# S4 convolution beside hedgehog linear attention on one core: state parameters and their power tables built in two halves of the channels

## The chip, the cores and the metric

The kernel runs on one core of a Trainium2 chip. The metric is the device time of one execution in microseconds (us). The median of three runs of the kernel before is 230.67 us. Five engines work side by side, each through its own list of instructions: TensorE (PE, matmuls and transposes), VectorE (DVE), ScalarE (ACT), GpSimd (POOL) and SyncE (SP), which here only issues DMAs. An instruction waits for the data and the buffers that it needs, and whatever stands behind it in the same engine's list waits with it.

## The reference

Two independent parts write side by side into an output of 2048 x 896 in bf16.

```python
# A: linear attention, 16 heads of 28, x is 2048 x 448
q, k, v = split(x @ wqkv)
phi(t) = concat(softmax(t @ w_phi), softmax(-(t @ w_phi)))
kv, z  = sum_s phi(k) v, sum_s phi(k)
a      = (phi(q) kv / (phi(q) z + 1e-6)) @ wo
# B: state space convolution, 448 channels d, 256 states n, u is 2048 x 448
dt     = exp(log_dt)
P      = exp(dt (A_re + i A_im) l),  l = 0..2047
K[d,l] = Re sum_n C[d,n] P[d,n,l] dt B[d,n]
y      = irfft(rfft(pad(u)) * rfft(pad(K)))[:2048] + u * Dskip
out    = concat(a, y)
```

## The kernel before, in words

Everything is tiled by hand. Code appends operations to a program (`prog.add`, engine letters E for PE, V for DVE, A for ACT, G for POOL, S for DMAs) and four lists at the end of the file decide the rest: ORDER is the order in which all 1040 operations are issued, so each engine's own order too; PLACES gives every SBUF buffer its address; SLOTS gives every PSUM use its bank (of eight); PICKS says for each copy, scaling or squaring whether ACT or DVE does it, and for each DMA whether it is issued on SP's queue or ACT's. No scheduler stands behind them. Buffers and banks are reused, so an operation that writes one waits for the readers of what lay there.

Part B has these stages. The 448 channels are taken in four quarters `qt` of 112 (224 columns, QC, for two groups of 128 states each; NCOL = 896 columns for all).

- Raw parameters: `load_raw` (L262) brings the six arrays A, B, C (real and imaginary) as 112 x 4 x 256, one DMA of 224 KB each; A_re goes on ACT's queue (L289). `Wqk` (L298) comes as one DMA and the constants of the signal spectrum, `G1` (L309), as another.
- States: `to_states` (L332) multiplies with the diagonal of dt on PE and lays states on partitions, into two PSUM banks. From A come AT and TH (decay and angle), from four products of C and B comes CR.
- Powers: for k in (128, 16, 8, 32, 64), `amp[k]` is an exponential on ACT, `cs[k]` two sines on ACT, and `PW[k]` their product on DVE, 1792 wide in f32. `PW[256]` is squared out of `q128`, and CB is CR times `PW[8]`. `K0` is a sum over CR for l = 0. All of it is done once, for all four quarters.
- Signal spectrum (`signal_spectrum(b)`, L420-440): PE reverses rows of u, ACT or DVE evacuates, DVE adds and subtracts (`ab`), PE multiplies with G1, ACT casts into `sg`, and a DMA stores it to DRAM (`SUd`, L249).
- Tables of a quarter (`tables(qt)`): `rotations` (sines) and `dampings` (exponentials) on ACT, `hi_tables`, `damp` and `far` on DVE, `build_k` on PE with casts by ACT or DVE, `scatter_k` by DMA through DRAM (`KTd`).
- `kernel_spectrum(qt)` on PE with casts, then `conv(qt)`: products on DVE, `finish` on DVE or `finish_pe` on PE, `inverse` on PE, an evacuation and a store to the output. The inverse of one `(qt, b)` makes two evacuations of 448 columns and two stores of 112 KB.

Part A (`fold_weights`, `key_side`, `query_side(sc)`) runs in between; its exponentials and evacuations are ACT's largest work, and x comes transposed by 16 DMAs on SP's queue (`dma_t`, L245). Sines and exponentials need different tables on ACT: where the list goes from the one to the other, a table load stands (L203 and L206). Helpers record all operations, so the profile shows their lines: L186 DVE tensor_tensor, L206 ACT activations, L214 copies and casts, L229 matmuls, L249 DMAs.

Of the kernel before, what the change touches and what calls it, by code (L numbers as in the profile page):

```python
# [10 lines left out]
F32 = mybir.dt.float32  # L11
ACT = mybir.ActivationFunctionType
ALU = mybir.AluOpType
# [116 lines left out]
def kernel(  # L130
# [116 lines left out]
    def dma(eng, o, i):  # L247
        e = {"S": nc.sync, "Q": nc.scalar}[prog.queue()]
        prog.add("S", lambda: e.dma_start(out=o, in_=i))  # L249
# [29 lines left out]
    def load_u(b):  # L279
# [9 lines left out]
    prog.add("S", lambda: nc.scalar.dma_start(  # L289
        out=raw["Are"].rearrange("p (u j) n -> p u (j n)", u=2),  # L290
        in_=srcs["Are"].rearrange("(u p j) n -> p u (j n)", u=2, j=2)))
    dma("S", PID, P_d)
    for nm in ("Aim", "Cre", "Bre", "Cim", "Bim"):
        load_raw(nm)
# [3 lines left out]
    Wqk = sb([112, 4, 2 * D_MODEL])  # L298
    WV = sb([128, 4, D_MODEL])
    dma("S", Wqk, wq3[:, :, 0:2 * D_MODEL])  # L300
# [8 lines left out]
    G1 = sb([128, 2, 4, 512])  # L309
    dma("S", G1, G_d)  # L310
# [12 lines left out]
    def from_states(bs):  # L323
        return view(psum[:, bs[0], 0:1], [512 * (bs[1] - bs[0]), 2], [56, 8], [1, 56])

    def by_states(v):
        return view(v, [56, 2], [112, 8], [1, 56])

    def to_states(bs, terms):
        items = []  # L330
        for j in range(4):
            for nch in range(2):  # L332
                at = 224 * (j // 2) + 56 * (j % 2)
                o = view(psum[:, bs[nch], at:at + 1], [112, 2], [1, 56])
                items += acc(o, [(t[:, j, 128 * nch:128 * nch + 128], d[:, j, :]) for t, d in terms])
        mms(items)

    AT = sb([128, 2, NCOL])
    TH = sb([128, 2, NCOL])
    bA, bT = prog.banks(2), prog.banks(2)  # L340
    for nm, b, dst in (("Are", bA, AT), ("Aim", bT, TH)):
        to_states(b, [(raw[nm], DG)])
        for nch in range(2):
            o0, o1 = (view(dst[:, part, 56 * nch:56 * nch + 1], [112, 8], [1, 2], [2, 28]) for part in range(2))
            i = view(psum[:, b[nch], 0:1], [56, 8], [28, 2], [1, 28])
            copy(o0, i)
            sub(o1, i, o0)
    prods = {}
    for a, b in (("Cre", "Bre"), ("Cim", "Bim"), ("Cre", "Bim"), ("Cim", "Bre")):
        prods[a + b] = sb([112, 4, SSM_N])  # L350
        mul(prods[a + b], raw[a], raw[b])

    LOWP = (128, 16, 8, 32, 64)
    PW = {k: sb([128, 2, NCOL]) for k in (8, 16, 32, 64, 128, 256)}
    amp = {k: sb([128, NCOL], F32) for k in LOWP}
    cs = {k: sb([128, 2, NCOL], F32) for k in LOWP}
    q128, q256 = (sb([128, 2, NCOL], F32) for _ in range(2))
    CR = sb([128, 2, NCOL])
    K0 = sb([128, D_MODEL])
    ones = sb([128, 128])  # L360
    for k in LOWP:
        af(by_states(amp[k]), from_states(bA), ACT.Exp, scale=float(k))
    for part, terms in enumerate(([("CreBre", DG), ("CimBim", DGN)], [("CreBim", DG), ("CimBre", DG)])):
        bs = prog.banks(2)
        to_states(bs, [(prods[n], d) for n, d in terms])
        copy(by_states(CR[:, part, :]), from_states(bs))
    mset(ones, 2.0 ** -17)
    (b_,) = prog.banks(1)
    mms([it for qt in range(4) for it in acc(
        view(psum[:, b_, 112 * qt:112 * qt + 1], [14, 8], [7, 2], [1, 7]),  # L370
        [(ones, view(CR[:, 0, QC * qt + 56 * nch:QC * qt + 56 * nch + 1], [7, 8], [112, 2], [1, 7]))
         for nch in range(2)])])
    copy(K0, psum[:, b_, 0:D_MODEL])
    for k in LOWP:
        af(by_states(cs[k][:, 0, :]), from_states(bT), ACT.Sin, scale=float(k), bias=bias_hp)
        af(by_states(cs[k][:, 1, :]), from_states(bT), ACT.Sin, scale=float(-k if k == 8 else k))
        mul(PW[k] if k != 128 else q128, cs[k], amp[k].unsqueeze(1).to_broadcast([128, 2, NCOL]))
        if k == 128:
            copy(PW[128], q128)
    s2 = sb([128, 2, NCOL], F32)  # L380
    square(s2, q128)
    sub(q256[:, 0, :], s2[:, 0, :], s2[:, 1, :])
    stt(q256[:, 1, :], q128[:, 0, :], -2.0, q128[:, 1, :], ALU.mult, ALU.mult)
    copy(view(PW[256][:, 0, 0:1], [56, 32], [1, 2], [2, 28]), view(q256[:, 0, 0:1], [56, 32], [28, 2], [1, 28]))
    CB = sb([128, 2, NCOL])
    TM = sb([128, 2, 2, NCOL])
    mul(TM, CR.unsqueeze(1).to_broadcast([128, 2, 2, NCOL]), PW[8].unsqueeze(2).to_broadcast([128, 2, 2, NCOL]))
    add(CB[:, 0, :], TM[:, 0, 0, :], TM[:, 1, 1, :])
    sub(CB[:, 1, :], TM[:, 0, 1, :], TM[:, 1, 0, :])
# [6 lines left out]
    def fold_weights(which):  # L396
        for cp in range(2):
            p = bank16(*prog.banks(1), [112, 2, D_MODEL])
            c0 = which * D_MODEL + 224 * cp
            transposes([(p[:, k, 112 * j:112 * j + 112], Wqk[:, j, c0 + 112 * k:c0 + 112 * k + 112], id112)  # L400
                        for k in range(2) for j in range(4)])
            copy(wT[:, which, 2 * cp:2 * cp + 2, :], p)
# [14 lines left out]
    def signal_spectrum(b):  # L417
# [9 lines left out]
        for cp in range(2):  # L427
            for st in range(2):
                k = 2 * cp + st
                sg = sb([128, 4, 4, 112])  # L430
                for mp in range(2):
                    items = []
                    bs = prog.banks(2)
                    for k2 in range(2):
                        mt = 2 * mp + k2
                        items += acc(psum[:, bs[k2], 0:D_MODEL],
                                     [(G1[:, cp, jt, 128 * mt:128 * mt + 128], ab[:, cp ^ st, jt, :])
                                      for jt in range(4)])
# [30 lines left out]
    def args(src, qt):  # L469
        cols = slice(qt * QC, (qt + 1) * QC)  # L470
# [8 lines left out]
    def rotations(qt):  # L479
        T = sb([128, 2, 7, QC])  # L480
        p0, far_ = args(TH, qt)
# [12 lines left out]
    def dampings(qt):  # L494
        A = sb([128, 21, QC])
        p0, far_ = args(AT, qt)
# [13 lines left out]
    def damp(W, A, T, qt, x0, w):  # L510
        scaled(A[:, 2:21:3, x0:x0 + w], A[:, 1:20:3, x0:x0 + w], -1.0)
        for part in (1, 0):
            copy(view(W[:, part, 1, x0:x0 + 1], [56, w // 56], [2, 28], [1, 2]),
                 view(PW[8][:, part, qt * QC + x0:qt * QC + x0 + 1], [56, w // 56], [1, 28], [28, 2]))
# [4 lines left out]
    def far(W, qt, x0, w):  # L519
        def pw(i, n):  # L520
            return view(PW[256][:, i, qt * QC + x0:qt * QC + x0 + 1], [0, 2], [0, n], [1, w])
# [14 lines left out]
        def squares(s0, ka, kb, d0):  # L536
# [3 lines left out]
            for i in range(2):  # L540
# [4 lines left out]
             PW[256][:, :, qt * QC + x0:qt * QC + x0 + w])  # L545
# [6 lines left out]
    def hi_tables(qt):  # L552
        cols = slice(qt * QC, (qt + 1) * QC)
# [5 lines left out]
        copy(U_[:, :, 0], CB[:, :, cols].rearrange("p i (s x) -> p s i x", x=28))  # L559
        for k, n, s0, d0 in ((16, 1, 0, 1), (32, 2, 0, 2), (64, 4, 0, 4)):  # L560
            t = sb([128, 2, 8, n, 2, 28])
            for i in range(2):
                times(t[:, i], U_[:, :, s0:s0 + n], PW[k][:, i, cols], 2 * n)
# [3 lines left out]
        for i, o in ((1, t), (0, U_[:, :, 8:16])):  # L567
            times(o, U_[:, :, 0:8], PW[128][:, i, cols], 16)
# [153 lines left out]
    def kernel_spectrum(qt, tiles):  # L722
        sk = SK[qt]
        for m in range(0, 8, 2):
            for b in range(2):
                (bk,) = prog.banks(1)
                items = []
                for cp in range(2):
                    for k in range(2):
# [3 lines left out]
                            halves(K0[:, 112 * qt:112 * qt + 112]),  # L733
# [8 lines left out]
    def conv(qt):  # L742
# [38 lines left out]
        def inverse(b, S):  # L781
            for r in range(2):
                (bk,) = prog.banks(1)
                items = []
                for jt in range(4):
                    items += acc(psum[:, bk, 112 * jt:112 * jt + 112],
                                 [(GI[:, r, cp, mt, 128 * jt:128 * jt + 128], S[:, r, cp, 112 * mt:112 * mt + 112])
                                  for cp in range(2) for mt in range(4)] + [(UT[:, b, r, 128 * jt:128 * jt + 128], DD[:, qt, :])])
                mms(items)
                OB = sb([128, 4, 112])  # L790
                copy(OB.rearrange("p t x -> p (t x)"), psum[:, bk, 0:D_MODEL])
                dma("S", rows(out2, b, r, D_MODEL + 112 * qt), OB)
# [142 lines left out]
```

## Time and profile before

| | |
|---|---|
| runs | 230.34, 230.67, 233.80 us, median 230.67 |
| the profiled execution | 231.53 us, span 229.8 us, mean granted PE clock 0.985 |
| table loads on ACT | 9 |
| DMA traffic in the trace | 32.87 MB, mean 143 GB/s |
| PE clock from 20 to 25 and 25 to 30 us | 0.76 and 0.56, else 1.00 |

A row of a timeline has the start and the length of a run of like instructions in us, the engine, the code line, the operation, output and input shapes, the count, and in brackets the idle time before it and what ended that. A row of a group has the count, then busy time and the mean ns of one, then the idle time before them. "PEld" is the weight load of PE, "SPq" and "ACTq" are the DMA issues of those queues.

### The profile page before, as it was taken

The numbers are of one execution on the slowest core, as the hardware profiler recorded it, in microseconds if no ns is written. First come the engines' busy times: TensorE is split into PE (matmuls) and PEld (weight loads), VectorE is DVE, ScalarE is ACT, GpSimd is POOL, SyncE is SP. The second block draws the span as 40 slices with busy tenths as digits, with TensorE's granted clock in tenths as the row PEclk, the third lists the DMA queues.
The fourth block names the chain that finished last, engine by engine and source line by source line (L and its number), as shares of the span: only waits on it lengthen the run. The fifth ranks groups of instructions, "written<-read, shape, count | busy, mean of one in ns | idle before, by whom it ended". The sixth has DMA issues, their size and how long they took to land.

```text
span 229.8 us, 7332 instructions
## 1 busy us (share of the span) xinstructions
PE 200.5 (87%) x3126; PEld 145.6 (63%) x3136; DVE 211.7 (92%) x269; ACT 192.5 (84%) x351; POOL 8.0 (3%) x26
## 2 busy tenths in 40 slices
PE   1154589999999899999887999999999999999993
PEld 1052246655557565787754868565676977799993
DVE  1499999999999899998999999999999989997991
ACT  2799999999999999999999999999798978235320
POOL 2000000001003000020100000010000000000000
PEclk9999599999999999999999999999999999999999
DMA  6992860969638999965576402414949863658842
GB/s 164 187 226 61 239 157 2 222 146 148 163 95 227 196 204 225 170 129 119 179 184 78 161 0 86 161 53 25 289 92 255 276 152 51 73 28 113 232 93 61
DMA packets 77608, 32.87 MB, mean 143 GB/s; under 512 B 64792, under 2 KB 75656, under 8 KB 77192
## 3 DMA queue, kind: packets, MB, share of 16 engines
q1 hardware_dynamic: 69864, 30.11, 60.0%
q10 hardware_dynamic: 7712, 2.31, 5.1%
q8 instruction: 24, 0.39, 0.7%
q14 instruction: 8, 0.07, 0.1%
HBM read 15.84 MB, written 8.49 MB: 106 GB/s over the span
## 4 chain that ended last, share of the span: by engine, by line
ACT 30%; DVE 27%; PE 24%; issue 8%; DMA 8%; DVEq 0%; ACTq 0%
PE psum L229 24%; DVE sbuf L186 24%; ACT sbuf L206 17%; ACT sbuf L214 10%; DMA sbuf<-in_B_C_re_dram 3%; DMA sbuf<-sbuf 2%; DVE sbuf L214 2%; DMA sbuf<-const 2%; DMA sbuf<-in_B_log_dt_dram 1%; ACT L203 1%; ACT L206 1%; ACT sbuf L220 1%; DVE sbuf L198 0%; DVE sbuf L217 0%; DVEq L186 0%
## 5 line engine op out<-in xcount | busy, mean ns | idle before, releaser
L229 PE MATMUL psum<-sbuf 128*128 128x112 bf16 (+9 forms) x3078 | 198.7, 256 | 25.1 <-DVE sbuf L186 12.7
L186 DVE TENSOR_TENSOR sbuf<-sbuf 128x896 bf16<-128x896 bf16 (+13 forms) x214 | 190.2, 947 | 8.9 <-ACT sbuf L206 3.8
L229 PEld LDWEIGHTS <-sbuf 128*128 128x128 bf16 (+5 forms) x3088 | 142.9, 112 | 78.6 <-issue 20.8
L214 ACT CAST sbuf<-psum 128x448 bf16<-128x448 f32 (+6 forms) x122 | 78.6, 701 | 24.8 <-PE psum L229 24.0
L206 ACT ACTIVATE sbuf<-psum 128x512 bf16<-128x512 f32 (+6 forms) x154 | 82.5, 628 | 2.3 <-PE psum L229 1.4
L206 ACT ACTIVATE sbuf<-sbuf 128x896 bf16<-128x896 bf16 (+3 forms) x29 | 18.9, 691 | 2.1 <-DMA sbuf<-in_B_log_dt_dram 1.2
L214 DVE CAST sbuf<-psum 128x448 bf16<-128x448 f32 (+3 forms) x21 | 13.3, 644 | 2.4 <-PE psum L229 2.4
L206 ACT ACTIVATE sbuf<-psum,sbuf 128x896 f32<-128x896 f32 (+3 forms) x17 | 13.9, 833 | 0.0
L224 POOL MEMSET sbuf<- 128x224 bf16 (+7 forms) x21 | 7.6, 397 | 144.0 <-PE psum L229 77.4
L214 ACT COPY sbuf<-psum 112x896 bf16<-112x896 bf16 (+2 forms) x11 | 7.0, 662 | 1.8 <-PE psum L239 1.8
L203 ACT ACT_TABLE_LOAD x5 | 6.4, 1283 | 1.6 <-PEq L919 1.3
L206 ACT ACT_TABLE_LOAD x4 | 5.1, 1283 | 1.8 <-DVE sbuf L186 1.7
L239 PEld LDWEIGHTS <-sbuf 112*112 112x112 bf16 (+1 forms) x48 | 3.1, 120 | 2.0 <-issue 1.7
L239 PE MATMUL psum<-sbuf 112*112 112x112 bf16 (+1 forms) x48 | 3.7, 216 | 0.7 <-DVE sbuf L186 0.6
L186 DVE TENSOR_TENSOR sbuf<-psum,sbuf 128x448 bf16<-128x448 f32 (+1 forms) x6 | 2.9, 489 | 0.6 <-PE psum L229 0.6
L214 DVE CAST sbuf<-sbuf 128x1792 bf16<-128x1792 f32 (+1 forms) x4 | 2.7, 696 | 0.5 <-ACT sbuf L206 0.5
L214 DVE COPY sbuf<-sbuf 128x448 bf16<-128x448 bf16 (+2 forms) x12 | 2.9, 261 | 0.0
L217 DVE TENSOR_SCALAR sbuf<-sbuf 128x1568 bf16<-128x1568 bf16 (+1 forms) x5 | 2.7, 547 | 0.0
L214 ACT COPY sbuf<-sbuf 128x224 bf16<-128x224 bf16 (+2 forms) x6 | 2.5, 424 | 0.0
L220 ACT ACTIVATE sbuf<-sbuf 128x1792 f32<-128x1792 f32 x1 | 1.8, 1795 | 0.0
L198 DVE SCALAR_TENSOR_TENSOR sbuf<-sbuf,psum 128x128 f32<-128x128 f32 x4 | 1.1, 282 | 0.1
L198 DVE SCALAR_TENSOR_TENSOR sbuf<-sbuf 128x896 f32<-128x896 f32 x1 | 1.1, 1079 | 0.0
(8 smaller groups left out, 1.9 us busy)
## 6 DMA issues: line engine op xcount, KB each, us to landing
SUd<-sbuf SPq DMA_DIRECT2D x8, 448.0 KB, 3.6
sbuf<-SUd SPq DMA_DIRECT2D x4, 896.0 KB
sbuf<-const SPq DMA_DIRECT2D x3, 1024.0 KB, 6.0
sbuf<-const SPq DMA_DIRECT2D x8, 384.0 KB, 4.0
sbuf<-in_B_u_dram SPq DMA_DIRECT2D x4, 448.0 KB
out_dram<-sbuf SPq DMA_DIRECT2D x10, 112.0 KB
out_dram<-sbuf SPq DMA_DIRECT2D x2, 448.0 KB, 2.8
out_dram<-sbuf ACTq DMA_DIRECT2D x2, 448.0 KB
```

The costliest lines, as they stand in the source:

```text
L186: prog.add("V", lambda: nc.vector.tensor_tensor(out=o, in0=a, in1=b, op=op))
L198: prog.add("V", lambda: nc.vector.scalar_tensor_tensor(out=o, in0=a, scalar=s, in1=b, op0=op0, op1=op1))
L203: nc.scalar.preload_act_table_set("natural_log_exp_and_others")
L206: nc.scalar.activation(o, a, fn, **kw)
L214: either(lambda: nc.scalar.copy(o, a), lambda: nc.vector.tensor_copy(o, a))
L217: either(lambda: nc.scalar.activation(o, a, ACT.Copy, scale=s), lambda: nc.vector.tensor_scalar_mul(o, a, s))
L220: either(lambda: nc.scalar.activation(o, a, ACT.Square), lambda: nc.vector.tensor_tensor(out=o, in0=a, in1=a, op=ALU.mult))
L224: prog.add("G", lambda: nc.gpsimd.memset(o, v))
L229: nc.tensor.matmul(o, lhsT=l, rhs=r, **kw)
L239: nc.tensor.transpose(o, i, idn)
```

## The change

1. The raw arrays are twelve buffers, `raw[u][nm]` of 112 x 2 x 256 for the halves u = 0 and 1 of the channels (quarters 0, 1 and 2, 3), each brought by a DMA of 112 KB. ORDER issues the six of u = 0 first, and those of u = 1 between and behind the loads of u, the transposes of x, the pieces of G1 and Wqk and five stores of the signal spectrum.
2. States, powers, CB and K0 are made by `powers(u)`, called for each half; a half has 448 columns where there were 896, and `to_states` fills one PSUM bank. In ORDER `powers(0)` stands at the start, and `powers(1)` is spread among the tables of quarters 0 and 1 and the key side. Users take `AT[qt // 2]` and so on.
3. `Wqk` comes in two DMAs (for k first, then q), `G1` in two.
4. The inverse of the last conv, `(qt, b) = (3, 1)`, is done in pieces of two column blocks: four evacuations of 224 columns and four stores of 56 KB.
5. ORDER, PLACES, SLOTS and PICKS are new throughout, with 1094 operations. PE has the same matmuls in the same shapes. DVE has 288 operations for 269, ACT 360 for 342 (table loads not counted). DVE casts four of the 1024-wide tiles (one before) and four of the 448-wide tiles of the kernel spectrum (eight before). Three transfers from KTd and one to it that were issued on ACT's queue are issued on SP's. Table loads on ACT are 11, with sines ahead of the first half's exponentials.

```diff
-    raw = {nm: sb([112, 4, SSM_N]) for nm in srcs}
-    def load_raw(nm):
-        dma("S", raw[nm].rearrange("p (u j) n -> p u (j n)", u=2), srcs[nm].rearrange("(u p j) n -> p u (j n)", u=2, j=2))
+    raw = [{nm: sb([112, 2, SSM_N]) for nm in srcs} for u in range(2)]
+    def raw_pair(nm, u):
+        return (raw[u][nm].rearrange("p j n -> p (j n)"),
+                srcs[nm].rearrange("(u p j) n -> u p (j n)", u=2, j=2)[u])
+    def load_raw(nm, u):
+        dma("S", *raw_pair(nm, u))
...
-    dma("S", Wqk, wq3[:, :, 0:2 * D_MODEL])
+    for which in (1, 0):
+        dma("S", Wqk[which], wq3[:, :, D_MODEL * which:D_MODEL * which + D_MODEL])
...
-    dma("S", G1, G_d)
+    for cp in range(2):
+        dma("S", G1[cp], G_d[:, cp])
...
+    def to_states(b, u, terms):
+        mms([it for j in range(2) for nch in range(2) for it in acc(
+            view(psum[:, b, 112 * j + 56 * nch:112 * j + 56 * nch + 1], [224, 2], [1, 56]),
+            [(t[:, j, 128 * nch:128 * nch + 128], d[:, 2 * u + j, :]) for t, d in terms])])
...
+    def powers(u):
+        (bA,), (bT,) = prog.banks(1), prog.banks(1)
+        for nm, b, dst in (("Are", bA, AT[u]), ("Aim", bT, TH[u])):
+            to_states(b, u, [(raw[u][nm], DG)])
...
+        for k in LOWP:
+            af(amp[k], psum[:, bA, 0:HC], ACT.Exp, scale=float(k))
...
+        for k in LOWP:
+            af(cs[k][:, 0, :], psum[:, bT, 0:HC], ACT.Sin, scale=float(k), bias=bias_hp)
+            af(cs[k][:, 1, :], psum[:, bT, 0:HC], ACT.Sin, scale=float(-k if k == 8 else k))
+            mul(PW[k][u] if k != 128 else q128, cs[k], amp[k].unsqueeze(1).to_broadcast([128, 2, HC]))
...
+    powers(0)
+    powers(1)
...
         def inverse(b, S):
+            n = 2 if (qt, b) == (3, 1) else 4
             for r in range(2):
-                (bk,) = prog.banks(1)
+                for j0 in range(0, 4, n):
+                    (bk,) = prog.banks(1)
...
-                dma("S", rows(out2, b, r, D_MODEL + 112 * qt), OB)
+                    dma("S", rows(out2, b, r, D_MODEL + 112 * qt)[:, j0:j0 + n], OB)
```

More of the change, by code (lines that the diff above doesn't have):

```diff
@@ L288 @@
     prog.add("G", lambda: nc.gpsimd.affine_select(eye, eye, [[-1, 112]], ALU.is_equal, 0.0, base=0, channel_multiplier=1))
-    prog.add("S", lambda: nc.scalar.dma_start(
-        out=raw["Are"].rearrange("p (u j) n -> p u (j n)", u=2),
-        in_=srcs["Are"].rearrange("(u p j) n -> p u (j n)", u=2, j=2)))
+    prog.add("S", lambda: nc.scalar.dma_start(out=raw_pair("Are", 0)[0], in_=raw_pair("Are", 0)[1]))
     dma("S", PID, P_d)
     for nm in ("Aim", "Cre", "Bre", "Cim", "Bim"):
-        load_raw(nm)
+        load_raw(nm, 0)
+    for nm in srcs:
+        load_raw(nm, 1)
     for i in range(4):
@@ L297 @@
     wq3 = A_wqkv.rearrange("(j p) n -> p j n", p=112)
-    Wqk = sb([112, 4, 2 * D_MODEL])
+    Wqk = [sb([112, 4, D_MODEL]) for which in range(2)]
     WV = sb([128, 4, D_MODEL])
-    dma("S", Wqk, wq3[:, :, 0:2 * D_MODEL])
+    for which in (1, 0):
+        dma("S", Wqk[which], wq3[:, :, D_MODEL * which:D_MODEL * which + D_MODEL])
     mset(WV[0:64, 3, :], 0.0)
@@ L308 @@
     prog.add("V", lambda: nc.vector.memset(bias_hp, PI / 2))
-    G1 = sb([128, 2, 4, 512])
-    dma("S", G1, G_d)
+    G1 = [sb([128, 4, 512]) for cp in range(2)]
+    for cp in range(2):
+        dma("S", G1[cp], G_d[:, cp])
     load_u(0)
@@ L321, in two @@
         return view(psum[0:parts, bs[0], 0:1], [512 * (bs[1] - bs[0]), 2], [1, D_MODEL])
[L323 to L336, printed above, removed]
@@ new lines @@
+    LOWP = (128, 16, 8, 32, 64)
+    HC = NCOL // 2
+    AT, TH, CR, CB = ([sb([128, 2, HC]) for u in range(2)] for _ in range(4))
+    PW = {k: [sb([128, 2, HC]) for u in range(2)] for k in (8, 16, 32, 64, 128, 256)}
+    K0 = [sb([128, D_MODEL // 2]) for u in range(2)]
+    ones = sb([128, 128])
+    mset(ones, 2.0 ** -17)
+    def powers(u):
+        (bA,), (bT,) = prog.banks(1), prog.banks(1)
+        for nm, b, dst in (("Are", bA, AT[u]), ("Aim", bT, TH[u])):
+            to_states(b, u, [(raw[u][nm], DG)])
+            o0, o1 = (view(dst[:, part, 0:1], [56, 8], [1, 2], [2, 28]) for part in range(2))
+            i = view(psum[:, b, 0:1], [56, 8], [28, 2], [1, 28])
@@ L346 @@
             copy(o0, i)
             sub(o1, i, o0)
[L348 to L389, printed above, removed]
+        prods = {}
+        for a, b in (("Cre", "Bre"), ("Cim", "Bim"), ("Cre", "Bim"), ("Cim", "Bre")):
+            prods[a + b] = sb([112, 2, SSM_N])
+            mul(prods[a + b], raw[u][a], raw[u][b])
@@ new lines, in powers @@
+        amp = {k: sb([128, HC], F32) for k in LOWP}
+        cs = {k: sb([128, 2, HC], F32) for k in LOWP}
+        q128, q256 = (sb([128, 2, HC], F32) for _ in range(2))
+        for k in LOWP:
+            af(amp[k], psum[:, bA, 0:HC], ACT.Exp, scale=float(k))
+        for part, terms in enumerate(([("CreBre", DG), ("CimBim", DGN)], [("CreBim", DG), ("CimBre", DG)])):
+            (b,) = prog.banks(1)
+            to_states(b, u, [(prods[n], d) for n, d in terms])
+            copy(CR[u][:, part, :], psum[:, b, 0:HC])
@@ new lines, in powers @@
+        (b_,) = prog.banks(1)
+        mms([it for q in range(2) for it in acc(
+            view(psum[:, b_, 112 * q:112 * q + 1], [14, 8], [7, 2], [1, 7]),
+            [(ones, view(CR[u][:, 0, QC * q + 56 * nch:QC * q + 56 * nch + 1], [7, 8], [112, 2], [1, 7]))
+             for nch in range(2)])])
+        copy(K0[u], psum[:, b_, 0:D_MODEL // 2])
+        for k in LOWP:
+            af(cs[k][:, 0, :], psum[:, bT, 0:HC], ACT.Sin, scale=float(k), bias=bias_hp)
+            af(cs[k][:, 1, :], psum[:, bT, 0:HC], ACT.Sin, scale=float(-k if k == 8 else k))
+            mul(PW[k][u] if k != 128 else q128, cs[k], amp[k].unsqueeze(1).to_broadcast([128, 2, HC]))
+            if k == 128:
+                copy(PW[128][u], q128)
@@ new lines, in powers @@
+        s2 = sb([128, 2, HC], F32)
+        square(s2, q128)
+        sub(q256[:, 0, :], s2[:, 0, :], s2[:, 1, :])
+        stt(q256[:, 1, :], q128[:, 0, :], -2.0, q128[:, 1, :], ALU.mult, ALU.mult)
+        copy(view(PW[256][u][:, 0, 0:1], [56, 16], [1, 2], [2, 28]), view(q256[:, 0, 0:1], [56, 16], [28, 2], [1, 28]))
+        TM = sb([128, 2, 2, HC])
+        mul(TM, CR[u].unsqueeze(1).to_broadcast([128, 2, 2, HC]), PW[8][u].unsqueeze(2).to_broadcast([128, 2, 2, HC]))
+        add(CB[u][:, 0, :], TM[:, 0, 0, :], TM[:, 1, 1, :])
@@ L391 @@
+        sub(CB[u][:, 1, :], TM[:, 0, 1, :], TM[:, 1, 0, :])
+    powers(0)
+    powers(1)
     wT = sb([112, 2, 4, D_MODEL])
@@ L398, in fold_weights @@
             p = bank16(*prog.banks(1), [112, 2, D_MODEL])
-            c0 = which * D_MODEL + 224 * cp
-            transposes([(p[:, k, 112 * j:112 * j + 112], Wqk[:, j, c0 + 112 * k:c0 + 112 * k + 112], id112)
+            c0 = 224 * cp
+            transposes([(p[:, k, 112 * j:112 * j + 112], Wqk[which][:, j, c0 + 112 * k:c0 + 112 * k + 112], id112)
                         for k in range(2) for j in range(4)])
```

56 lines of the change are left out of this document (25 added, 31 removed), and 112 rows, old and new, of tables (ORDER, PLACES, SLOTS).

## The prediction

> **What bounds the kernel now.** I read the page's totals first, then five stretches of the span, then the waits of each engine, then the timelines of the head and the tail, where the edits lie.
>
> ```profile
> PE 200.5 (87%) x3126; PEld 145.6 (63%) x3136; DVE 211.7 (92%) x269; ACT 192.5 (84%) x351; POOL 8.0 (3%) x26
> ```
> ```profile
> 0.00:15.00 15.00, 2.46 (x26) 2.33 (x26) 7.05 (x14) 9.18 (x12) 1.50 (x9) 1.00 0.91 187
> 15.00:35.00 20.00, 13.46 (x77) 8.01 (x75) 20.00 (x22) 19.97 (x29) 0.00 (x0) 0.83 0.63 157
> 35.00:160.00 125.00, 118.85 (x1776) 80.37 (x1784) 123.11 (x159) 123.09 (x235) 6.54 (x17) 1.00 0.63 137
> 160.00:200.00 40.00, 39.39 (x755) 29.55 (x753) 39.23 (x53) 30.95 (x61) 0.00 (x0) 1.00 0.68 169
> 200.00:230.00 30.00, 26.30 (x508) 25.31 (x505) 22.32 (x25) 9.35 (x19) 0.00 (x0) 1.00 0.63 104
> ```
> The columns are length, then busy time of PE, PE's weight loads, DVE, ACT and POOL, then the PE clock, DMA share and GB/s. DVE is the bound: it is idle 15 − 7.05 = 7.95 us in the first 15 us, never between 15 and 35 us, and 1.89 + 0.77 us between 35 and 200. ACT is as full up to 160 us (idle 5.82 us before 15 us, then 1.94), and has slack after. PE is idle 12.54 + 6.54 = 19.08 us before 35 us, 6.15 in the next 125, 0.61 up to 200. Three engines are near their limit at once, so what one gains in the head counts only if the other two can take it.
>
> ```profile
> ACT sbuf L214 <- PE psum L229: 24.0, 15, 4.8
> DVE sbuf L186 <- ACT sbuf L206: 3.8, 2, 3.1
> DVE sbuf L186 <- DMA sbuf<-in_B_C_re_dram: 2.5, 1, 2.5
> DVE sbuf L214 <- PE psum L229: 2.4, 2, 1.4
> ```
> ```profile
> 6.41 1.19 DVE L214 CAST sbuf<-psum 128x448 bf16<-128x448 f32 x2 [1.43 <-PE psum L229]
> 10.64 0.69 DVE L186 TENSOR_TENSOR sbuf<-sbuf 112x1024 bf16<-112x1024 bf16 x1 [2.50 <-DMA sbuf<-in_B_C_re_dram]
> 15.20 13.76 DVE L186 TENSOR_TENSOR sbuf<-sbuf 128x1792 bf16<-128x1792 f32 x9
> ```
> ```profile
> 5.57 0.65 ACT L214 CAST sbuf<-psum 128x448 bf16<-128x448 f32 x1 [1.63 <-PE psum L229]
> 6.09 4.16 ACT L206 ACTIVATE sbuf<-psum 128x896 f32<-128x896 f32 x5
> 11.97 1.28 ACT L206 ACT_TABLE_LOAD   x1 [1.72 <-DVE sbuf L186]
> ```
> ```profile
> 14.18 4.66 PE L229 MATMUL psum<-sbuf 112*128 112x112 bf16 x40 [7.81 <-DVE sbuf L186]
> 29.10 4.84 PE L229 MATMUL psum<-sbuf 128*128 128x448 bf16 x24 [0.20 <-DVE sbuf L186]
> ```
> So 2.50 us of DVE's idle is the wait for the C arrays, and 1.43 and 1.63 us (DVE, ACT) are the wait for the first state matmuls. PE waits 7.81 us for the products, and the signal spectrum's dense run begins at 29.10, behind the 13.76 us in which DVE works off the full-width power products.
>
> **The change, term by term.** All of it is counted on DVE, with ACT and PE beside it.
>
> *Head: −3.3 us.* The first halves are six loads of 112 KB instead of six of 224 KB, so the products have their operands after half of the bytes: at 187 GB/s (the first window row) the 672 KB that no longer stand ahead are 0.69 MB / 187 = 3.7 us. That covers the 2.50 us wait, and the first product, ready then, fills about 0.8 of the 1.43 us. I take 7.95 − 3.3 = 4.65 us of idle left (bounds 4.0 to 7.15: only the 1.43 row unfilled and half the load wait gone, or nearly all of both filled; the 3.1 us in the wait on ACT's exponential of log_dt stays, as that load is not changed). ACT's idle goes from 5.82 to about 2.5, since its list now begins with sines, whose table is loaded while it waits for the first matmuls (−1.72), and they start on half a matmul set (−1.6). The lists put the signal spectrum's sums of u behind five half-width products instead of behind the whole 13.76 us, so PE's dense run comes about 8 us earlier, at about 21 us.
>
> *More instructions on DVE: +0.9.*
> ```profile
> L186 DVE TENSOR_TENSOR sbuf<-sbuf 128x896 bf16<-128x896 bf16 x74 | 43.4, 617 | 0.4
> L186 DVE TENSOR_TENSOR sbuf<-sbuf 128x448 bf16<-128x448 bf16 x16 | 5.8, 381 | 0.0
> L186 DVE TENSOR_TENSOR sbuf<-sbuf 128x1792 bf16<-128x1792 f32 x4 | 7.8, 2010 | 0.0
> L214 DVE CAST sbuf<-sbuf 128x1792 bf16<-128x1792 f32 x2 | 2.2, 1137 | 0.0
> L214 DVE CAST sbuf<-psum 128x448 bf16<-128x448 f32 x17 | 10.4, 620 | 2.4 <-PE psum L229 2.4
> L214 DVE CAST sbuf<-psum 128x1024 bf16<-128x1024 f32 x1 | 1.2, 1215 | 0.0
> ```
> ```profile
> 192.88 2.22 DVE L186 TENSOR_TENSOR sbuf<-sbuf 128x896 bf16<-128x896 bf16 x4
> ```
> Instructions overlap: four of 896 take 2.22 us, so one starts (2.22 − 0.617) / 3 = 0.534 us after the other, 0.083 less than its duration. A 448 then costs 0.381 − 0.083 = 0.298, and two of them 0.06 more than one 896. Some fourteen instructions become two each (the five full-width f32 products, the two 896 f32 ones of q256, the four products of C and B, those of CB): 14 × 0.06 = 0.9.
>
> *Two f32 casts half given to ACT: −1.0.* Two of 1.137 − 0.083 = 1.05 us become four halves, of which two stand on ACT.
>
> *Evacuations picked anew: +2.9.* DVE takes four of the 1024-wide casts instead of one, 3 × (1.215 − 0.083) = +3.4; four of the 448-wide spectrum casts instead of eight, 4 × 0.537 = −2.1; a dozen smaller moves (an 896 more, two 320 fewer, three 224 copies more and the like) by widths between these rows come to +1.6.
>
> DVE's work: +0.9 − 1.0 + 2.9 = +2.8 us.
>
> *ACT: about +3.*
> ```profile
> L206 ACT ACT_TABLE_LOAD x4 | 5.1, 1283 | 1.8 <-DVE sbuf L186 1.7
> L214 ACT CAST sbuf<-psum 128x1024 bf16<-128x1024 f32 x8 | 8.0, 1068 | 0.9 <-PE psum L229 0.8
> ```
> ```profile
> 72.29 0.59 ACT L206 ACTIVATE sbuf<-psum 128x448 bf16<-128x448 f32 x1
> 72.89 1.28 ACT L206 ACT_TABLE_LOAD   x1
> 74.19 1.01 ACT L206 ACTIVATE sbuf<-psum,sbuf 128x896 bf16<-128x896 f32 x1
> 92.52 1.42 ACT L214 CAST sbuf<-psum 128x448 bf16<-128x448 f32 x3
> ```
> In the head ACT's list goes from sines to exponents and back to sines, which needs two more table loads, eleven for nine: 2 × 1.28 = 2.57 us; the second half's sines stand beside those of quarter 1 and need none. The fifteen 896-wide f32 activations become thirty of 448: from the rows 92.52 and 6.09, three 448s take 1.42 us and five 896s take 4.16, so that each further one adds (1.42 − 0.57) / 2 = 0.43 and (4.16 − 0.95) / 4 = 0.80 us: 15 × (0.86 − 0.80) = 0.9. Two half casts add 1.6, and the evacuations that DVE takes, less those ACT takes, give back about 2. It is paid by the 3.3 us of the head, so ACT stands even at 160 us and hides nothing more after; if its head gain is missing, each us of it delays evacuations up to 160 us.
> By the Trainium skill (ScalarE: Activation LUTs, What ACT_TABLE_LOAD costs; its rules ask to finish one table set before the next) a switch is 1283 ns plus a drain of about 1380. The trace agrees on the load and not on the drain: the instruction before ends at 72.88, the load runs to 74.17, the next starts at 74.19. By the Trainium skill's figure ACT's term would be 2.75 us larger.
>
> *Raw loads, Wqk and G1 in pieces, and their place on SP's queue: 0, bounds 0 and +8 (rival three).* The second half's loads and their matmuls, products and powers are needed only by quarters 2 and 3; what covers them is the work of quarters 0 and 1 on all three engines. Four KTd transfers go from ACT's queue to SP's, at about 0.4 us of issue each (the SP rows under rival three), where SP stands idle between issues.
>
> *The split end: −0.4.*
> ```profile
> 195.75 30.55 PE L229 MATMUL psum<-sbuf 128*128 128x112 bf16 x568 [0.40 <-DVE sbuf L214]
> 209.81 13.21 DVE L186 TENSOR_TENSOR sbuf<-sbuf 128x3584 bf16<-128x3584 bf16 x13 [1.55 <-ACT sbuf L214]
> 224.57 0.62 DVE L214 CAST sbuf<-psum 128x448 bf16<-128x448 f32 x1 [1.01 <-PE psum L229]
> 226.34 0.53 ACT L214 CAST sbuf<-psum 128x448 bf16<-128x448 f32 x1 [4.02 <-PE psum L229]
> ```
> After the last matmul comes a 448-wide evacuation of 0.53 us and a store to the end at 229.8. With 224 columns the evacuation is about 0.2 us shorter and the store carries half; I take 0.4 (bounds 0.1 and 0.7), less nothing for the two more stores, which start earlier.
>
> *Stalls: −0.8.* DVE is busy 211.7, idle 7.95 in the head and 229.8 − 225.19 = 4.6 behind its last instruction, so 229.8 − 211.7 − 7.95 − 4.6 = 5.55 us are stalls behind the head; 1.55 and 1.01 are the tail's rows above. PE's earlier run shortens the tail's waits for it. Against that stand new waits of the second half with its single banks: a cast of its Are states waits for the sines of quarter 1, which read the same bank. I take 0.8 off (bounds −5.5 and +2).
>
> **Sum:** −3.3 + 2.8 − 0.4 − 0.8 = −1.7, 228.1 us of span. The profiled execution took 231.53 us at a span of 229.8, so 229.8 after; the runs' median is 230.67, 0.86 under that execution, which gives **229.0 us**.
>
> **Rivals.**
>
> *One, faster: PE's gain is carried through.* PE recovers up to 8 of its 19.08 us of idle, the tail's run of 568 matmuls starts earlier, and DVE's 5.55 us of stalls fall to about 1: 229.8 − 3.3 + 2.8 − 0.4 − 4.6 = 224.3 of span, 225.2 as a median. For it: ACT waits 24.0 us for PE, most in the tail, and DVE's own waits for PE are 2.4. Against it: DVE works without a gap in most stretches, so PE can't run ahead of what DVE hands it, and 0.61 us of PE idle between 160 and 200 is all that is to be had there.
>
> *Two, no gain: ACT becomes the bound.* ACT's +3 us aren't paid by the head (the sines still wait for PE), and delay evacuations up to 160 us: 230.67 + 2.6 − 0.4 = 232.9. It decides when less than half of ACT's 3.3 us is gained. For it: 1.94 us of slack in 125. Against it: three 1024-wide casts (1.07 us each) leave ACT. Where DVE's head gain is lost with it, it is 230.67 + 2.8 + 2.6 − 0.4 = 235.7. By the Trainium skill's figure for a switch (that page and section) 232.9 would be 235.6.
>
> *Three, slower: the second half comes late on SP's queue.*
> ```profile
> 5.92 1.94 SPq L249 DMA_DIRECT2D sbuf<-in_B_u_dram  x3
> 21.10 0.36 SPq L249 DMA_DIRECT2D sbuf<-const  x1
> 39.22 0.41 SPq L249 DMA_DIRECT2D SUd<-sbuf  x1
> 59.14 0.59 SPq L249 DMA_DIRECT2D sbuf<-in_A_wqkv_dram  x1
> ```
> SP issues in order. The last half array (the imaginary part of C) stands about 45th on it, behind five stores of the spectrum, each waiting for an ACT cast, and most of the transposes of x. Before, the queue stood from 7.86 to 21.10 and to 39.22, and reached such a place only at 59.14. DVE's list wants the product at about 56.4 us (4.65 of idle + 51.7 of work ahead of it). If the queue is no earlier than before, the load lands near 59.7 + 3 and the rows behind the stores push it to 64: DVE stands about 8 us at that product, 229.0 + 8 = 237. It goes past 2% from 6.3 us late on. Against it: the stores wait for casts that come 8 us earlier, so the load should be issued near 45 us and wait for nobody.
>
> **Chances.** Forecast 0.44 (its own range 226.5 to 231.5), rival one 0.27, rival two 0.12 (0.03 of it past 2%), rival three 0.17. 2%, about what a measurement of this kernel can tell from no change, is 4.6 us: faster below 226.06 is rival one, 0.27; slower above 235.28 is 0.17 + 0.03 = 0.20; within is 0.44 + 0.09 = 0.53. The range reaches from 224.6 (0.05 of rival one below it) to 235.4 (0.15 of rival three above).
>
> **What would show it.** Right: no DVE row with a wait on the C arrays, DVE's first 15 us busy near 10.3; the 448-wide spectrum matmuls beginning near 21 us; DVE's total near 214.5 and eleven table loads; the last evacuation 224 wide. Wrong: a DVE or PE wait on a raw array between 50 and 70 us (rival three), ACT without a gap while DVE and PE wait on its casts before 160 us (rival two), DVE's stalls behind the head under 2 us (rival one), or a head whose 3.3 us are eaten by a new wait for the spectrum's constants.

## The result and the profile after

The changed kernel takes 266.59 us (median of four runs, 266.32 to 266.88) where the kernel before, run beside it, takes 230.77 (four runs, 230.34 to 233.80): 1.156 times the time, 95% interval 1.1535 to 1.1585. Some executions of a kernel are over 1.5% longer than its fastest; the times and ratios of the experiments below leave those out, and each ratio is to the kernel before run beside it, with its 95% interval in brackets. The profiled execution has a span of 265.1 us. First its totals and its windows, the latter with the same columns as those of before:

```profile
PE 211.0 (80%) x3128; PEld 148.7 (56%) x3136; DVE 216.9 (82%) x288; ACT 200.7 (76%) x371; POOL 8.0 (3%) x26
```
```profile
0.00:15.00 15.00, 4.11 (x29) 2.82 (x30) 10.68 (x20) 12.81 (x20) 1.54 (x8) 1.00 0.98 187
15.00:35.00 20.00, 14.18 (x63) 7.16 (x62) 14.74 (x29) 13.79 (x22) 0.78 (x3) 1.00 0.61 155
35.00:160.00 125.00, 99.67 (x1348) 66.44 (x1351) 103.43 (x135) 106.54 (x205) 5.12 (x13) 0.96 0.55 125
160.00:200.00 40.00, 34.47 (x526) 22.29 (x527) 33.79 (x42) 32.38 (x59) 0.51 (x2) 1.00 0.27 60
```

The head is what the prediction said: DVE is busy 10.68 us of the first 15. Right behind it all three engines fall back together. Between 35 and 160 us DVE is busy 103.43 us where it was busy 123.11, ACT 106.54 where it was 123.09, PE 99.67 where it was 118.85. No engine is the bound any more; each waits for another. The groups of waits say for whom (total, times, longest, in us):

```profile
ACT sbuf L214 <- PE psum L229: 36.6, 36, 3.4
DVE sbuf L186 <- ACT sbuf L206: 19.7, 7, 5.5
PE psum L229 <- ACT sbuf L214: 19.4, 20, 2.4
ACT sbuf L206 <- PE psum L229: 12.6, 14, 3.1
PE psum L229 <- ACT sbuf L206: 11.2, 10, 2.1
DVE sbuf L214 <- ACT sbuf L214: 7.2, 4, 2.5
```

Before, the groups of that kind, beside the 24.0 us of the first one, were small:

```profile
PE psum L229 <- ACT sbuf L214: 7.5, 6, 3.0
ACT sbuf L206 <- PE psum L229: 1.4, 2, 0.9
PE psum L229 <- ACT sbuf L206: 1.1, 4, 0.5
```

ACT waits 36.6 + 12.6 = 49.2 us for PE where it was 24.0 + 1.4 = 25.4, and PE waits 19.4 + 11.2 = 30.6 us for ACT where it was 8.6. That is the pattern to look for: two engines that take turns. The timeline from 34 to 54 us, in the signal spectrum, shows one turn after the other:

```profile
34.76 3.19 PE L229 MATMUL psum<-sbuf 128*128 128x448 bf16 x16
...
37.23 0.91 ACT L214 CAST sbuf<-psum 128x896 bf16<-128x896 f32 x1 [1.31 <-PE psum L229]
...
41.28 0.97 ACT L214 CAST sbuf<-psum 128x896 bf16<-128x896 f32 x1
...
42.30 2.48 PE L229 MATMUL psum<-sbuf 128*128 128x448 bf16 x8 [2.44 <-ACT sbuf L214]
...
44.81 1.71 ACT L214 CAST sbuf<-psum 128x896 bf16<-128x896 f32 x2 [2.30 <-PE psum L229]
...
48.80 0.95 ACT L214 CAST sbuf<-psum 128x896 bf16<-128x896 f32 x1
...
49.80 1.67 PE L229 MATMUL psum<-sbuf 128*128 128x448 bf16 x8 [1.25 <-ACT sbuf L214]
51.51 0.91 ACT L214 CAST sbuf<-psum 128x896 bf16<-128x896 f32 x1 [0.91 <-PE psum L229]
...
52.47 2.07 PE L229 MATMUL psum<-sbuf 128*128 128x448 bf16 x16 [0.99 <-ACT sbuf L214]
53.30 4.24 DVE L186 TENSOR_TENSOR sbuf<-sbuf 128x896 bf16<-128x896 bf16 x6 [5.52 <-ACT sbuf L206]
```

Now the banks, which SLOTS and ORDER give for each of these operations. The 896-wide casts read two PSUM banks in one instruction, a step of 512 x (b1 - b0) elements apart (`two`, L326).

| row | engine | its banks | it waits for | whose banks are |
|---|---|---|---|---|
| 42.30 | PE | 2 and 3 | the cast at 41.28, ends 42.25 | 0 and 4 |
| 44.81 | ACT | 1 and 6 | the matmuls at 42.30, end 44.78 | 2 and 3 |
| 49.80 | PE | 1 and 7 | the cast at 48.80, ends 49.75 | 0 and 3 |
| 52.47 | PE | 2 and 3 | the cast at 51.51, ends 52.42 | 1 and 7 |

In no row do the two share a bank. But in each, at least one of PE's banks lies between the two of the cast: the read is ordered as if it covered every bank from its first to its last. The matmuls on banks 1 and 6, which the cast at 44.81 reads, are among the 16 at 34.76 and ended by 37.95; the cast stood 2.30 us for matmuls on banks that it does not read, and PE had stood 2.44 us before that for a cast that does not read them either. DVE's 5.52 us at 53.30 is a wait for ACT's squares, which stand behind these casts on ACT's list.

How many such pairs there are can be counted in the text of SLOTS, where a two-digit word is a two-bank use. Before, all 48 are neighbours; after, 36 of 44 are not:

```
before  67 01 45 23 67 67 23 45 45 67 01 01 67 23 23 45 23 01 01 45 67 01 01 01 ...
after   07 46 17 26 17 23 16 26 57 04 67 07 15 23 07 26 03 23 15 23 07 46 23 04 ...
```

With them 41 reads span banks that they do not use, and 38 waits between engines join operations without a bank in common; before there is none of either. The waits are semaphores that the program carries, since that is what the trace infers a releaser from; kernel.py sets none itself. So this is an ordering that the layer beneath the kernel puts into the program. Whether the chip would need it was not tested.

### The profile page after: what moved, and what is told of

Its sections match the earlier page's. It is cut to its first block, busy times and chain, and to the rows that moved or that the text cites. A ratio compares the mean times of both kernels' runs of the same rounds, so it can differ in the third digit from the quotient of the medians.

```text
span 265.1 us, 7378 instructions
## 1 busy us (share of the span) xinstructions
PE 211.0 (80%) x3128; PEld 148.7 (56%) x3136; DVE 216.9 (82%) x288; ACT 200.7 (76%) x371; POOL 8.0 (3%) x26
## 5 line engine op out<-in xcount | busy, mean ns | idle before, releaser
L229 PE MATMUL psum<-sbuf 128*32 128x80 bf16 (+8 forms) x3080 | 208.2, 260 | 49.5 <-ACT sbuf L214 19.4
L186 DVE TENSOR_TENSOR sbuf<-sbuf 128x896 bf16<-128x896 bf16 (+13 forms) x227 | 192.3, 902 | 22.3 <-ACT sbuf L206 16.5
L229 PEld LDWEIGHTS <-sbuf 128*128 128x128 bf16 (+4 forms) x3088 | 145.3, 114 | 110.7 <-issue 56.3
L214 ACT CAST sbuf<-psum 128x448 bf16<-128x448 f32 (+8 forms) x127 | 77.7, 643 | 41.5 <-PE psum L229 36.6
L214 DVE CAST sbuf<-psum 128x448 bf16<-128x448 f32 (+4 forms) x21 | 15.4, 747 | 12.1 <-ACT sbuf L214 5.6
L206 ACT ACTIVATE sbuf<-psum,sbuf 128x448 f32<-128x448 f32 (+3 forms) x22 | 14.2, 682 | 1.6 <-PE psum L229 1.6
L214 DVE COPY sbuf<-sbuf 128x448 bf16<-128x448 bf16 (+2 forms) x16 | 5.4, 340 | 0.0
L214 ACT CAST sbuf<-sbuf 128x896 bf16<-128x896 f32 (+1 forms) x3 | 2.6, 876 | 0.0
L214 DVE CAST sbuf<-sbuf 128x192 bf16<-128x192 f32 (+1 forms) x5 | 2.0, 407 | 0.3 <-ACT sbuf L206 0.3
L220 ACT ACTIVATE sbuf<-sbuf 128x896 f32<-128x896 f32 x2 | 1.9, 950 | 0.0
```

The lines of the kernel that those rows point to most:

```text
L186: prog.add("V", lambda: nc.vector.tensor_tensor(out=o, in0=a, in1=b, op=op))
L206: nc.scalar.activation(o, a, fn, **kw)
L214: either(lambda: nc.scalar.copy(o, a), lambda: nc.vector.tensor_copy(o, a))
L220: either(lambda: nc.scalar.activation(o, a, ACT.Square), lambda: nc.vector.tensor_tensor(out=o, in0=a, in1=a, op=ALU.mult))
L229: nc.tensor.matmul(o, lhsT=l, rhs=r, **kw)
```

## The experiments

Theory: the far pairs make the loss. Rivals: the loss is the change's own (order of work, halves, evacuations); it sits in the signal spectrum alone; it comes from ACT's two more table loads; it is the work given to DVE. In the expectations theory one is the far pairs, theory two the new order and picks, theory three the second half of the raw arrays coming late. "Drawn anew" means that SLOTS alone differs: each PSUM use has another bank, ORDER, PLACES, PICKS and all instructions stay.

**Far pairs taken out of the changed kernel, two ways.** First SLOTS drawn anew with every pair adjacent:

```diff
-    "6 0 1 2 6 1 3 4 0 7 1 1 07 46 17 26 17 23 16 26 57 04 67 07 4 7 15 ...
+    "5 1 4 0 2 7 3 4 6 7 6 3 34 01 67 12 34 45 67 45 01 23 01 45 7 0 01 ...
```

> The changed kernel with SLOTS alone drawn anew, so that each two-bank evacuation reads banks that lie side by side, as all 48 did before (36 of 44 lie apart in the changed kernel). Order, places and picks are those of the changed kernel. Theory one (a read of two banks that lie apart also waits for what PE writes into the banks between them, and PE for it): 225 to 232 us, waits of ACT on PE and of PE on ACT back to those of before, spectrum steps 1.4 to 1.7 us apart. Theory two (the new order and the picks themselves alternate PE and ACT): 258 us or more. Theory three (the second half of the raw arrays comes late): about 262, with DVE still idle between 48 and 61 us.

Measured: 235.06 us, 1.013 times before [1.0094, 1.0164]; theory one, though some 3 us above its range. Then its own SLOTS kept, and each two-bank read issued as one instruction per bank (50 instructions more, for the 41 far reads and nine whose banks are neighbours):

```diff
-            copy(ur[:, 2 * tp:2 * tp + 2, :], two(bs))
+            copy2([ur[:, 2 * tp + k, :] for k in range(2)], [psum[:, bs[k], 0:D_MODEL] for k in range(2)])
```

> The changed kernel with its own SLOTS; only the 41 two-bank reads are issued as two instructions, one for each bank, so nothing spans a bank between. Theory one: 228 to 237 us, since 41 more instructions cost 0.05 to 0.2 us each on ACT and DVE, most of which shows. Theory two and three: 264 us or more, as order and banks are unchanged.

Measured: 235.78 us, 1.013 [1.0075, 1.019]. Here every bank is where the change put it, and some 31 us are gone. Theories two and three, which said 264 us or more, fall. Its totals, and the stretch that was shown above (matmuls and copies stand on L234 and L215 there):

```profile
PE 201.8 (86%) x3128; PEld 145.2 (62%) x3136; DVE 215.9 (92%) x293; ACT 200.2 (85%) x416; POOL 8.4 (4%) x26
```
```profile
38.62 16.97 PE L234 MATMUL psum<-sbuf 128*128 128x448 bf16 x108 [0.42 <-ACT sbuf L215]
```

Where PE took turns with ACT, it runs 16.97 us without a gap.

**Far pairs put into the kernel before.** Its banks renamed 0 to 7 as 0, 4, 1, 5, 2, 6, 3, 7, so that all 48 pairs lie apart; nothing else.

```diff
-    "67 01 45 23 5 6 7 67 67 23 45 45 67 01 01 ...
+    "37 04 26 15 6 3 7 37 37 15 26 26 37 04 04 ...
```

> The kernel before with the eight PSUM banks renamed (0, 4, 1, 5, 2, 6, 3, 7 for 0 to 7) and nothing else: reuse of banks, order, picks and places are the same, but all 48 pairs lie apart. Theory one: 255 to 310 us, with ACT waiting for PE and PE for ACT in the signal spectrum. Theory two and three: 231 us, as nothing that they rest on is changed.

Measured: 280.87 us, 1.208 [1.2008, 1.2148]. A renaming leaves the reuse of every bank as it was, so this 20.8% is the far pairs and nothing else. In the timeline the turns are plain; each matmul group waits for a cast and each cast for a matmul group:

```profile
30.91 0.91 PE L229 MATMUL psum<-sbuf 128*128 128x448 bf16 x2 [4.01 <-ACT sbuf L206]
31.85 0.91 ACT L214 CAST sbuf<-psum 128x896 bf16<-128x896 f32 x1 [0.75 <-PE psum L229]
32.81 0.91 PE L229 MATMUL psum<-sbuf 128*128 128x448 bf16 x2 [0.99 <-ACT sbuf L214]
33.75 0.91 ACT L214 CAST sbuf<-psum 128x896 bf16<-128x896 f32 x1 [0.99 <-PE psum L229]
...
34.71 1.28 PE L229 MATMUL psum<-sbuf 128*128 128x448 bf16 x3 [0.99 <-ACT sbuf L214]
35.65 0.92 ACT L206 ACTIVATE sbuf<-psum 128x896 bf16<-128x896 f32 x1 [0.99 <-PE psum L229]
```

**Far pairs made nearer.** The changed kernel with its banks renamed 0 to 7 as 3, 0, 7, 6, 4, 1, 5, 2: the banks that lie between the two of a pair, summed over all pairs, fall from 110 to 49, 22 pairs lie apart instead of 36, and 15 of the 38 waits are left.

> The changed kernel with its banks renamed (3, 0, 7, 6, 4, 1, 5, 2 for 0 to 7): reuse, order, picks and places are those of the changed kernel, but the pairs span 49 banks between them instead of 110. Theory one (waits on the banks between): 236 to 246 us, between the changed kernel and the one with pairs side by side. Theories two and three: 264 us or more, since names do nothing.

Measured: 241.21 us, 1.043 [1.0384, 1.0484]. A renaming alone takes 25 of the 36 us away.

**Is it the signal spectrum alone?** Its 20 two-bank reads were issued per bank. Of these 15 are far, as SLOTS shows, so 26 of the 41 far reads stay (the 21 of the expectation is a miscount), and 26 of the 38 waits.

> The changed kernel with its own SLOTS, and only the signal spectrum's 20 two-bank evacuations issued as one instruction for each bank (21 others still span banks). If the loss lies in the spectrum's ping-pong between 24 and 66 us: 238 to 248 us. If it is spread over the rotations, dampings and query side as well: 250 us or more.

Measured: 256.92 us, 1.111 [1.1042, 1.1176]. Some 10 of the 31 us go. The rest sits with the other far reads: the rival falls.

**Controls on the kernel before.** Its reads issued per bank (67 instructions more), and its SLOTS drawn anew with adjacent pairs.

> The kernel before with each two-bank read issued as two instructions: a control for the price of splitting alone. All theories: 232 to 239 us, 63 more instructions or so at 0.05 to 0.2 us on ACT, which is full up to 160 us.

Measured: 235.97 us, 1.016 [1.0101, 1.0224].

> Control: the kernel before with its SLOTS drawn anew by the same recipe, all two-bank uses adjacent as they were. If a new drawing by itself costs what is left over before in the changed kernel (1.3 to 2.8%), this one lies 1 to 3% above before. If it lies within 0.5% of before, the drawings are no worse than the one that the kernel before has, and what is left in the changed kernel is its own.

Measured: 235.07 us, 1.015 [1.0119, 1.0189]. Both controls matter: what the edits cost by themselves is as large as what is left over in the changed kernel.

**More drawings of the changed kernel**, all with adjacent pairs.

> The changed kernel with a second drawing of SLOTS in which all pairs lie side by side, other banks reused later than in the first. What is left over the kernel before (1.3% in the first drawing) lies either in the drawing (reuse of single banks): then 229 to 232 us here; or in the change's own work, order and picks: then 233 to 236 us again.

Measured: 237.45 us, 1.028 [1.0223, 1.033], above both of its ranges.

> The changed kernel with a third drawing of its SLOTS: every two-bank use on adjacent banks again, and the banks chosen so that a single-bank use is taken up again as late as can be. Two other such drawings gave 1.013 and 1.028 times the kernel before. Theory A (pair gaps cost the 15.6%, and what is left over them is the reuse of banks, not the change itself): this drawing is at or below the better of the two, 1.00 to 1.013 times before, 230 to 234 us. Theory B (what is left is the change's own, its order of work and its extra evacuations on VectorE): 1.013 to 1.03, whatever the drawing. The forecast of 0.993 for the change would stand only if this comes out under 1.00.

Measured: 234.85 us, 1.012 [1.0077, 1.0156].

> A fourth drawing of the same kind (all two-bank uses adjacent), made like the third from another start. It shows how far two drawings made alike lie apart: theory A gives 1.00 to 1.013 again, theory B 1.013 to 1.03. If the third and fourth lie more than 1% apart, single drawings can't tell a term of 0.7%.

Measured: 234.69 us, 1.014 [1.0088, 1.0196]. Four drawings give 1.012 to 1.028, and the first, third and fourth lie within 0.3%. None is below 1.00, and the control drawn by the same recipe is at 1.015. By themselves the four lie in the range of theory B as well as near that of theory A. It is the control that speaks for A: a new drawing alone costs the kernel before as much as three of the four leave over in the changed kernel. That all of what is left over is the drawing is not shown.

**Table loads.** The second drawing, with the first half's five exponentials, and the PE operation that feeds them, ahead of its sines in ORDER, so that ACT loads nine tables and not eleven.

> The same, with the first half's five exponentials put ahead of its sines on ACT's list (and the states of A_re ahead of them on PE's), so that two table loads go: nine again instead of eleven. If the two loads are on the path (ACT is full up to 160 us): 1 to 2.6 us less than the second drawing. If ACT's head idle hides them: within 0.5 us of it. If DVE's first power products, which then wait longer for their sines, are on the path: up to 1 us more.

Measured: 237.47 us, 1.028 [1.0233, 1.0318], against 237.45 for the same drawing without the edit. The time stays, but the edit does two things. The first windows, second drawing above, with the edit below:

```profile
0.00:15.00 15.00, 5.34 (x35) 3.75 (x36) 10.66 (x20) 12.79 (x20) 1.54 (x8) 1.00 0.95 188
0.00:15.00 15.00, 3.31 (x25) 2.29 (x26) 6.81 (x14) 9.65 (x17) 1.54 (x8) 1.00 0.94 191
```

ACT is spared two loads (2.57 us), and DVE, whose products now wait for their sines, loses 10.66 - 6.81 = 3.85 us of its first 15. So the run does not price the loads alone. It shows that the two effects together change nothing that can be measured, and that table loads do not make the loss.

**The casts given to DVE.** The third drawing, with three of the four 1024-wide casts given back to ACT.

```diff
-            copy(OT[:, 2 * cp:2 * cp + 2, :], view(psum[:, bs[2 * cp], 0:1], ...
...
+            if (sc, cp) == (3, 1):
+                prog.add("V", lambda ot=ot: nc.vector.tensor_copy(*ot))
+            else:
+                prog.add("A", lambda ot=ot: nc.scalar.copy(*ot))
```

> The third drawing, and the three 1024-wide casts of the linear attention that the change moved from ScalarE to VectorE moved back (VectorE keeps one, as before the change). VectorE's work falls by 3 x 1.13 = 3.4 us, ScalarE's grows by 3 x 1.07 = 3.2. If VectorE's queue is what ends the stretches (the forecast's reading, by which these casts cost 3.4 us): 2 to 3.4 us faster than the third drawing, about 0.99 of it. If ScalarE's casts are what the other two engines wait for: no gain or up to 3 us slower.

Measured: 237.47 us (two executions), 1.025 [1.0208, 1.0294], so 1.013 times the third drawing, give or take 0.006. In its profiled execution, a longer one of 241.64 us, DVE's busy time falls from 215.3 to 211.9 us, ACT's grows from 197.3 to 200.2, and the kernel gets slower. ORDER was not made anew for it, so it does not show what the best place for these casts is; it shows that a us taken off DVE was not a us gained.

No version beats the kernel before.

## Why the prediction was wrong

It forecast 229.0 us, chances 0.27, 0.53 and 0.20 for faster, the same and slower; it is 266.59, far out of the range of 224.6 to 235.4. All in profiled executions, on DVE, with idle time split as the prediction split it (first 15 us; behind DVE's last instruction; the rest, called stalls):

| term, us | forecast | after less before | third drawing less before drawn anew |
|---|---|---|---|
| head, idle of the first 15 us | -3.3 | 4.32 - 7.95 = -3.6 | 4.29 - 7.00 = -2.7 |
| DVE's work | +2.8 | 216.9 - 211.7 = +5.2 | 215.3 - 212.5 = +2.8 |
| end and stalls | -0.4 and -0.8 | 43.9 - 10.15 = +33.7 | 13.5 - 14.9 = -1.4 |
| span | -1.7 | 265.1 - 229.8 = +35.3 | 233.1 - 234.4 = -1.3 |

**The step that failed is "Stalls: -0.8 (bounds -5.5 and +2)".** DVE's stalls rose from 5.55 to 265.1 - 216.9 - 4.3 - 3.5 = 40.4 us. The prediction looked at waits that the new order adds and named one bank conflict, Are against the sines of quarter 1; it took "SLOTS is new" to be free beyond that. The prediction worked through each engine's queue, and no queue by itself shows that two engines take turns. What it needed was in the text of SLOTS, 36 far pairs; what such a pair costs no row of the kernel before could show, as all its pairs are neighbours. Each such wait can cost about one cast (0.91 us, row 37.23) or one group of eight matmuls (1.67 us, row 49.80), and more where the other engine has work ahead of it (2.44 us, row 42.30); at 0.91 to 1.67 us the 38 of them are an estimate of 35 to 63 us if none is hidden, so the upper bound of +2 had no ground.

**With the far pairs out, on equal terms, the other terms stand.** The last column compares two kernels with SLOTS from the same recipe. Their totals and first windows:

```profile
PE 203.5 (87%) x3128; PEld 145.9 (63%) x3136; DVE 215.3 (92%) x288; ACT 197.3 (85%) x371; POOL 8.4 (4%) x26
```
```profile
0.00:15.00 15.00, 5.37 (x34) 3.67 (x35) 10.71 (x21) 12.84 (x21) 1.54 (x8) 1.00 0.93 189
15.00:35.00 20.00, 17.56 (x92) 9.44 (x91) 19.87 (x34) 19.50 (x32) 0.78 (x3) 1.00 0.58 153
35.00:160.00 125.00, 113.43 (x1737) 77.30 (x1740) 121.66 (x152) 122.55 (x240) 6.12 (x15) 0.99 0.65 141
```

The third drawing stands above, the kernel before drawn anew below.

```profile
PE 202.4 (86%) x3126; PEld 145.9 (62%) x3136; DVE 212.5 (91%) x269; ACT 193.6 (83%) x351; POOL 7.8 (3%) x26
```
```profile
0.00:15.00 15.00, 3.42 (x36) 3.28 (x37) 8.00 (x15) 10.12 (x13) 1.50 (x9) 1.00 0.92 194
15.00:35.00 20.00, 13.84 (x65) 7.29 (x63) 20.00 (x21) 19.95 (x29) 0.00 (x0) 0.74 0.63 152
35.00:160.00 125.00, 116.95 (x1752) 78.94 (x1760) 121.01 (x158) 121.01 (x230) 6.31 (x17) 1.00 0.65 136
```

The ratio of their times is 1.0117 / 1.0154 = 0.996, give or take 0.005 (half intervals of 0.0039 and 0.0035, added as squares). The pair with reads per bank gives 1.0133 / 1.0163 = 0.997, give or take 0.008, and 1.001 if the control is charged only 50 of its 67 extra instructions. These margins hold for single pairs of drawings; the four drawings of the changed kernel against the one control give 0.996 to 1.012. The forecast was 0.993. So the change itself, apart from its banks, is within 2% of no change, as forecast; whether it gains the 0.7%, gains nothing or loses a little, these runs do not tell.

Step by step:

- Head, right as idle time. The waits on the C arrays are gone; what is left of DVE's idle in the changed kernel is three rows, 0.87 + 2.73 + 0.68 = 4.3 us:

```profile
0.87 0.06 DVE L313 MEMSET sbuf<- 128x1 f32 x1 [0.87 <-PEq L926]
3.66 0.63 DVE L186 TENSOR_TENSOR sbuf<-sbuf 112x448 bf16<-112x448 bf16 x1 [2.73 <-ACT sbuf L206]
...
5.28 0.66 DVE L214 CAST sbuf<-psum 128x448 bf16<-128x448 f32 x1 [0.68 <-PE psum L229]
```

  Whether these us are worth as much in time is not shown: in the experiment on table loads 3.85 us of DVE's head were lost again, with two loads fewer on ACT, and the time stayed.
- PE's earlier start, right and in part given back. In the changed kernel its 448-wide run of 24 begins at 24.06 us where it was 29.10 (about 21 was forecast), itself behind a wait for a cast. On equal terms the dense run begins 7.8 us earlier, at 21.34 us in the third drawing and at 29.14 in the control (the kernel before drawn anew). The three rows, in that order:

```profile
24.06 7.30 PE L229 MATMUL psum<-sbuf 128*128 128x448 bf16 x24 [1.05 <-ACT sbuf L214]
...
21.34 7.06 PE L229 MATMUL psum<-sbuf 128*128 128x448 bf16 x32 [0.97 <-ACT sbuf L214]
...
29.14 10.39 PE L229 MATMUL psum<-sbuf 128*128 128x448 bf16 x48 [0.50 <-ACT sbuf L206]
```

  The wait for a constant that the prediction named as a danger is there, on PE and not on DVE, 4.49 us in the changed kernel and 3.27 in the third drawing:

```profile
13.83 2.42 PE L229 MATMUL psum<-sbuf 128*128 128x448 bf16 x10 [4.49 <-DMA sbuf<-const]
```

  In the third drawing PE has 35 - 22.93 = 12.1 us of idle before 35 us against 17.7 in the control, and between 35 and 160 us it has 11.6 against 8.1: of 5.7 us gained, 3.5 are lost again behind the head. That fits rival one's own counterargument, that PE can't run ahead of what DVE hands it.
- DVE's work, +2.8 on equal terms as forecast; +5.2 in the changed kernel.
- ACT, +3.7 on equal terms where about 3 was forecast, with eleven table loads. A load after an instruction again costs its 1.28 us and no more:

```profile
76.99 1.99 ACT L206 ACTIVATE sbuf<-psum 128x448 bf16<-128x448 f32 x4
79.00 1.28 ACT L206 ACT_TABLE_LOAD   x1
80.30 0.54 ACT L206 ACTIVATE sbuf<-psum 128x448 bf16<-128x448 f32 x1
```

  The activation before ends at 78.98 and the next starts 0.02 us behind the load, so the drain of about 1380 ns that the Trainium skill (ScalarE: Activation LUTs, What ACT_TABLE_LOAD costs) adds to a switch is not seen here either.
- "DVE is the bound", too simple. Three casts taken off DVE and put on ACT made the kernel 1.3% slower. Up to 160 us ACT has as little slack as DVE (2.45 and 3.34 us idle in the third drawing's 125). That a cast late on ACT then holds PE's banks, as rival two has it, fits this but was not shown by itself.
- Split end, right. From PE's end to the span's end it is 3.50 us before (226.30 to 229.8), 3.23 in the third drawing (229.87 to 233.1), 3.12 with reads per bank, so about 0.3 of the 0.4 forecast; the last evacuation is 224 wide and takes 0.34 us.
- Rival three, wrong in kind although the side was right. The last half array is issued late, at 60.72 us, as that rival had it:

```profile
60.09 0.53 SPq L249 DMA_DIRECT2D SUd<-sbuf  x1
60.72 0.45 SPq L249 DMA_DIRECT2D sbuf<-in_B_C_im_dram  x1
```

  But the stores ahead of it were late since the casts were, and DVE's waits around it are for ACT (5.52 us at 53.30); none is for a raw array.

## What to carry to other kernels

When a kernel's banks are given anew, look at the pairs that one instruction reads: banks that lie apart in one access pattern were ordered here against every bank between them, and that alone cost 13% (266.6 against 235.1 us) to 21%. Where neighbours can't be had, one instruction per bank is free of it; here it cost 1.6% in the kernel before, for 67 more instructions. And compare a new layout with the old kernel in a new layout by the same recipe: here that control moved by 1.5%, more than the change that was to be measured.

## What the runs showed of the hardware

The Trainium skill (PSUM — Partial Sum Buffer, PSUM bank collisions raise a hardware error) asks for semaphores by bank and quadrant and says that two engines on different banks run clean. The waits seen here, which the program carries, go further, by the range from the first to the last bank of a read: with one instruction per bank, at the same banks, they are gone and 31 us with them.

The same matmuls, in the same shapes, are busy 211.0 us in the changed kernel and 211.4 in the kernel before with its pairs apart, and 200.5 to 203.5 where they follow one another closely (before, third drawing), while the mean granted clock is 0.980, 0.976, 0.985 and 0.992 in these four. What of that is a matmul that is longer after a gap and what is the clock was not measured apart.

The choice of banks has a price of its own even when all pairs are neighbours: the four drawings of the same program differ by up to 1.6%, and the kernel before loses 1.5% with the same instructions in the same order, by its banks alone.
